# Batch 0 of a scan-then-FFN kernel taken as two tokens per partition and left unsorted, with prologue and block 0 reordered

## The chip, the cores and the metric

The kernel runs on one core of a Trainium2 chip. The metric is the device time of one execution in microseconds (us). A time is 1.7 to 2.3 us longer than the span of the same execution in the profile, because the span runs from the first to the last recorded instruction. "Fast" runs are those that are not in a slower state of the chip; all comparisons here use fast runs.

## The reference, cut to what matters

Two stages follow each other: a chunked state-space scan (batch 4, 8 heads, 768 tokens, head width 32, state width 16), and a gated feed-forward network (FFN) on its result (3072 tokens of width 256, inner width 1536).

```python
for c in range(nc):                                  # chunks in order
    cum = np.cumsum(log_a_chunk);  L = np.exp(cum_i - cum_j) * causal
    y_intra = ((C_chunk @ B_chunk.T) * L) @ x_chunk
    y_inter = (C_chunk @ state) * np.exp(cum)
    state   = np.exp(sum(log_a_chunk)) * state + (B_chunk * decay).T @ x_chunk
...
out = (np.maximum(y @ w_gate, 0) * (y @ w_val)) @ w_out
```

The kernels use chunks of 128 tokens, which gives the same result.

## The kernel before

The 3072 tokens are 12 pairs of chunks (256 tokens each, three pairs per batch) and 6 FFN blocks of 512 tokens. While block b goes through the FFN, the attention of pairs 2b+2 and 2b+3 is prepared between its matmuls. The FFN takes 12 columns f of 128: two gate and two value matmuls, a ReLU on ACT, a product h on DVE; then four output groups `fout` of 12 matmuls. A half step `gvh` takes one column for 256 tokens, a whole step `gv` for 512.

Every engine runs strictly in the order of the program text: a last pass chains each instruction to the one before it on its engine. So an instruction that waits holds up all that stands behind it on that engine. The eight PSUM banks are `y`, `Aps` (the state), `tp` (transposes) and five shared ones.

Pairs 0 to 3 are loaded "wide", with two neighbouring tokens in each partition, so that B and C come in packets of 128 bytes. Permutation matmuls then sort them back to one token per partition. The other pairs are loaded "narrow".

```python
    def sort_wide(p, engs=None, own=False):          # 8 matmuls and 2 copies for a wide pair
        ...
            for r in range(2):
                nc.tensor.matmul(out=o[:, 0:128], lhsT=order[:, i, r], rhs=s["tin"][0][r], ...)
                nc.tensor.matmul(out=o[:, 128:384]..., lhsT=order[:, i, r], rhs=s["xw"][:, r], ...)

    def tevac(p, beng, ceng):                        # B and C, transposed, leave the bank tp
        tp = s.pop("tp")
        ...
        (beng.copy if beng is nc.scalar else beng.tensor_copy)(rows(BT), tokens(0))   # first: B on ACT
        ...
        nc.vector.tensor_tensor(out=out_, in0=src.to_broadcast(shape),                # then: C on DVE
                                in1=mk.to_broadcast(shape), op=ALU.mult)
...
    # prologue: the 64x384 scan for all decays, then pair 0, then pair 1's transposes
    turn(0, True); tevac(0, nc.scalar, nc.vector); sort_wide(0, ...); G(0); gevac(0, half=False); state(0, 0)
    weights(4, 8); load(2, ...); load(3, ...); scale_bc(1, nc.vector); cast_x(1, nc.scalar); keep_warm(7)
    Dm(0); inter(0, 1); astep(0, 1); yevac(0, nc.scalar)
    turn(1, True); tevac(1, nc.scalar, nc.vector); sort_wide(1); sevac(0, 1)

    for b in range(NBLK):
        P, Q, W = 2 * b + 2, 2 * b + 3, 2 * b + 1
        ...
        for f in range(4):
            gvh(b, f, 0)
            if b == 0 and f == 0:
                G(1); gevac(1); state(1, 0); weights(8, NF); wait_for(2, 1); weights_out(0, NF)
            if f == (3 if b == 0 else 1):
                ... inter(W, 0); inter(W, 1); Dm(W); ... yevac(W, nc.scalar)
        for f in range(4):
            gvh(b, f, 1)
        for f in range(4, NF):
            gv(b, f)
            if at("scale P", 4, 4, 4): scale(P, nc.gpsimd, nc.gpsimd)     # columns for blocks 0, 1, 2 and later
            if at("turn P", 7, 6, 5):  turn(P); tevac(P, nc.scalar, nc.vector)
            if at("state P0", 9, 8, 7): state(P, 0)
            if at("turn Q", 99, 9, 8): turn(Q); tevac(Q, nc.scalar, nc.scalar)
            ...
        # output groups fout(b, 0..3), with G, gevac, Dm, yevac of P and G, gevac of Q between them
```

Of the kernel before, what the change touches and what calls it, by code (L numbers as in the profile page):

```python
# [29 lines left out]
def kernel(  # L30
# [13 lines left out]
    nc = tc.nc  # L44
# [27 lines left out]
    NWIDE = 4  # L72
    st = {}

    def wide_bc(p, qb, qc):
        b, c0 = p // PPB, 2 * (p % PPB)
        sl = slice(c0 * 128, (c0 + 2) * 128)
        bcr = raw.tile([128, NH, 2, 2, N], FP32, tag="bcr", name="bcr")
        for src, j, q in ((C, 1, qc), (B, 0, qb)):
            if (p, j) in ((0, 0), (2, 1)):  # L80
                nc.vector.memset(bcr[0:1, 0, 0, 0, 0:1], 0.0)  # L81
            q.dma_start(
                out=bcr[:, :, j].rearrange("p h r n -> p h (r n)"),
                in_=src[b, :, sl, :].rearrange("h (p r) n -> p h (r n)", r=2))
        st.setdefault(p, {})["bcr"] = bcr

    def wide_x(p, *qs):

        b, c0 = p // PPB, 2 * (p % PPB)
        sl = slice(c0 * 128, (c0 + 2) * 128)  # L90
        xr = raw.tile([128, NH, 2, D], FP32, tag="xr", name="xr")
        n = NH // len(qs)
        for k, q in enumerate(qs):
            hs = slice(k * n, (k + 1) * n)
            q.dma_start(out=xr[:, hs].rearrange("p h r d -> p h (r d)"),
                        in_=x[b, hs, sl, :].rearrange("h (p r) d -> p h (r d)", r=2))
        st.setdefault(p, {})["xr"] = xr

    def load(p, qx, qb, qc):
        b, c0 = p // PPB, 2 * (p % PPB)  # L100
        if p < NWIDE:
            wide_bc(p, qb, qc)
            wide_x(p, qx)
        else:
            xr = raw.tile([128, 2, NH, D], FP32, tag="xr", name="xr")
            bcr = raw.tile([128, 2, 2, NH, N], FP32, tag="bcr", name="bcr")
            for i in range(2):
                sl = slice((c0 + i) * 128, (c0 + i + 1) * 128)
                qx.dma_start(out=xr[:, i], in_=x[b, :, sl, :].rearrange("h s d -> s h d"))
                for src, j, q in ((B, 0, qb), (C, 1, qc)):  # L110
                    q.dma_start(out=bcr[:, i, j],
                                in_=src[b, :, sl, :].rearrange("h s n -> s h n"))
            st[p] = {"xr": xr, "bcr": bcr}

    H = S // 2
    HC = NC // 2
    a_sb = glob.tile([2 * BH, H], FP32)
    nc.sync.dma_start(out=a_sb, in_=a.rearrange("b h (w s) -> (b h w) s", w=2))
    first = const.tile([1, 2], FP32)
    nc.vector.memset(first, 0.0)  # L120
    nc.scalar.activation(first[:, 1:2], first[:, 0:1], AF.Relu)


    warm = const.tile([128, 512], BF16)
    nc.vector.memset(warm, 0.0)
    wide_bc(0, nc.scalar, nc.sync)
    wide_x(0, nc.sync, nc.scalar)
    wide_bc(1, nc.scalar, nc.sync)
    wide_x(1, nc.sync)
# [3 lines left out]
    make_identity(nc, ident)  # L133
    maskUT = const.tile([128, 1, 128], BF16)
    make_upper_triangular(nc, maskUT[:, 0], 1.0, diag=True)
# [4 lines left out]
    bd = const.tile([128, 128], BF16)  # L140
    nc.vector.memset(bd, 0.0)
    smask = const.tile([128, 2, 128], BF16)
    for k in range(4):
        nc.vector.memset(bd[32 * k:32 * k + 32, 32 * k:32 * k + 32], 1.0)
        nc.vector.memset(tmask[32 * k:32 * k + N, 0:1], 1.0)
    nc.vector.tensor_scalar(out=tmask[:, 1:2], in0=tmask[:, 0:1], scalar1=-1.0,
                            scalar2=1.0, op0=ALU.mult, op1=ALU.add)
    for t in range(2):
        nc.vector.tensor_scalar_mul(smask[:, t], bd, tmask[:, t:t + 1])
    pick = const.tile([2 * BH, 2, BH], FP32)  # L150
    pairs = identf.rearrange("p (h w) -> p w h", w=2)
    nc.vector.tensor_copy(pick[:, 1], pairs[:, 1])
    order = const.tile([128, 2, 2, 128], BF16)
    nc.gpsimd.memset(order, 0.0)
    for r in range(2):
        nc.gpsimd.tensor_copy(
            order[:, :, r].rearrange("p c (m r) -> p c m r", r=2)[:, :, :, r],
            ident.rearrange("p (c m) -> p c m", c=2))

    def keep_warm(n):  # L160
        w = bank("w")
        for _ in range(n):
            nc.tensor.matmul(out=w, lhsT=warm[:, 0:128], rhs=warm, start=True, stop=True)  # L163

    keep_warm(8)


# [15 lines left out]
    gate = const.tile([1, 4], FP32)  # L183

    def wait_for(p, j):

        nc.gpsimd.tensor_copy(gate[:, 2 * j:2 * j + 1], st[p]["bcr"][0:1, 0, j, 0, 0:1])

    wait_for(0, 1)
    weights(0, 4)  # L190


    cp = glob.tile([2 * BH, H], FP32)
    nc.vector.tensor_tensor_scan(
        out=cp, data0=a_sb, data1=zero1.to_broadcast([2 * BH, H]), initial=1.0,
        op0=ALU.mult, op1=ALU.add)
    rmid = const.tile([2 * BH, 1], FP32)
    nc.vector.reciprocal(rmid, cp[:, H - 1:H])
    nc.vector.tensor_scalar_mul(pick[:, 0], pairs[:, 0], rmid)

    def wide_decay(ps):

        d = bank("wdec", (128, len(ps), 2, 8))
        first = True
        for k, p in enumerate(ps):
            b, c0 = p // PPB, 2 * (p % PPB)
            for i in range(2):
                w, o = (c0 + i) // HC, ((c0 + i) % HC) * 128
                for r in range(2):
                    nc.tensor.matmul(  # L210
                        out=d[64 * i:64 * i + 64, k, r],
                        lhsT=cp[:, o + r:o + 128:2], rhs=pick[:, w, 8 * b:8 * b + 8],
                        start=first or (k == 0 and r == 0), stop=True,
                        tile_position=(0, 64 * i), skip_group_check=True)
                first = False
        return d

    def wide_factors(ps, d):
        f = const.tile([128, len(ps), 2, 2, 8], FP32, name="wf%d" % ps[0])
        nc.vector.reciprocal(f[:, :, 0], d)  # L220
        nc.vector.tensor_copy(f[:, :, 1], d)
        for k, p in enumerate(ps):
            st[p]["f"] = f[:, k].rearrange("p j r h -> p (j r) h")
# [22 lines left out]
    A_ps = mm.tile([128, 2, 128], FP32, tag="Aps", name="A_ps")  # L246

# [4 lines left out]

    def scale_bc(p, eng):
# [3 lines left out]
        if p < NWIDE:  # L257
            src = s["bcr"].rearrange("s (t q) j r n -> s (j r) t q n", t=2)
            f = s["f"]
        else:  # L260
            src = s["bcr"].rearrange("s i j (t q) n -> s (i j) t q n", t=2)
            f = scaleBC[:, b, c0:c0 + 2].rearrange("s c j h -> s (c j) h")
# [6 lines left out]
        if p < NWIDE:  # L269
            s["tin"] = [[bs[:, 2 * j + r] for r in range(2)] for j in range(2)]  # L270
        else:
            s["tin"] = [[bs[:, 2 * i + j] for i in range(2)] for j in range(2)]
            s["B"] = s["tin"][0]

    def cast_x(p, ceng):
# [3 lines left out]
        if p < NWIDE:  # L279
            cast(xb, s["xr"].rearrange("s h r d -> s (h r d)"))  # L280
            s["xw"] = xb.rearrange("s (h r d) -> s r h d", h=NH, r=2)
        else:
            cast(xb, s["xr"].rearrange("s i h d -> s (i h d)"))
            s["x"] = [xb[:, i * NH * D:(i + 1) * NH * D] for i in range(2)]

    def sort_wide(p, engs=None, own=False):

        s = st[p]
        bx = att.tile([128, 2, 384], BF16, tag="bx", name="bx")
        for i in range(2):  # L290
            if own and i == 0:
                o = mm.tile([128, 384], FP32, tag="y", name="bxp")
            else:
                o = bank("bxp", (128, 384))
            for r in range(2):
                nc.tensor.matmul(out=o[:, 0:128], lhsT=order[:, i, r], rhs=s["tin"][0][r],
                                 start=(r == 0), stop=(r == 1), skip_group_check=True)
                nc.tensor.matmul(
                    out=o[:, 128:384].rearrange("s (h d) -> s h d", h=NH),
                    lhsT=order[:, i, r], rhs=s["xw"][:, r],  # L300
                    start=False, stop=(r == 1), skip_group_check=True)
            eng = engs[i] if engs else nc.scalar
            (eng.copy if eng is nc.scalar else eng.tensor_copy)(out=bx[:, i], in_=o)
        s["B"] = [bx[:, i, 0:128] for i in range(2)]
        s["x"] = [bx[:, i, 128:384] for i in range(2)]
# [14 lines left out]
    def tevac(p, beng, ceng):  # L320
# [7 lines left out]
        def tokens(k, lead=""):  # L328
            src = tp[k]
            if wide:  # L330
                return src.rearrange("s r m -> s m r")
            return src.rearrange("s i m -> s (i m)")

        def rows(dst):
            dst = dst.rearrange("s i m -> s (i m)")
# [57 lines left out]
    def astep(p, i):  # L393

        c = 2 * (p % PPB) + i
        if c == NC - 1:
            return
# [260 lines left out]
```

## Time and profile before

| | before |
|---|---|
| time, two runs | 133.66 us (133.47 and 133.84) |
| span of the profiled run | 132.1 us |
| start to the first gate matmul | 13.56 us |
| from there to block 0's first output matmul | 16.88 us |
| from there to block 1's first output matmul | 19.40 us |
| from there to the end | 82.26 us |

The page's row of busy times (share of the span, instructions):

```profile
PE 125.6 (95%) x1150; PEld 83.3 (63%) x1157; DVE 90.1 (68%) x196; ACT 81.7 (62%) x177; POOL 37.6 (29%) x76
```

The page's chain that ended last, as shares of the span:

```profile
PE 58%; DVE 1%; issue 0%; DVEq 0%
```

Hardly any other engine is in the chain. The view follows it back only as far as 50.63 us (59% of the span), so for what lies before that the windows have to be read. That PE bounds the kernel there too is seen from how little it idles. The windows view, cut at the four moments of the table (stretch, its length, then busy time and instructions of each engine, granted clock, DMA share, rate):

```profile
core 0: us, PE busy (x) PEld busy (x) DVE busy (x) ACT busy (x) POOL busy (x), PEclk, DMA share, GB/s
0.00:13.56 13.56, 12.13 (x86) 6.15 (x88) 8.48 (x36) 5.40 (x11) 6.88 (x20) 1.00 0.97 140
13.56:30.44 16.88, 15.62 (x135) 9.31 (x133) 12.93 (x28) 11.03 (x27) 7.05 (x12) 1.00 1.23 178
30.44:49.84 19.40, 19.35 (x193) 13.51 (x192) 13.69 (x28) 13.89 (x32) 5.43 (x10) 1.00 0.83 115
49.84:132.10 82.26, 78.51 (x746) 54.31 (x747) 55.04 (x107) 51.42 (x111) 18.29 (x34) 1.00 0.34 60
```

Length less PE's busy time is what PE idled: 1.43, 1.26, 0.05 and 3.75 us. In the third stretch, from block 0's output to block 1's, it idles practically never. PE's longest waits besides the start are accordingly short (waits view: engine, line, what released it: us in total, times, longest):

```profile
PE gv L478 <- ACT yT L448: 0.5, 1, 0.5
PE y L424 <- DVE Sm L406: 0.3, 1, 0.3
```

What a wide pair costs on PE, from the timeline (start, us, engine, line, operation, out<-in, shapes, count). A group's end overlaps the next group's start, so the distance from one start to the next is its cost:

```profile
33.72 0.22 PE L296 MATMUL bxp<-bs,order 128*128 128x128 bf16 x1
...
34.38 1.47 PE L490 MATMUL o<-wo,h 128*128 128x256 bf16 x12
35.78 0.41 PE L435 MATMUL y<-gs,bx 128*32 128x128 bf16 x16
36.12 0.40 PE L361 MATMUL g<-CT,BT 32*128 32x256 bf16 x8
```

The sort costs 34.38 − 33.72 = 0.66 us, the 16 diagonal matmuls 0.34, and the 8 score matmuls 0.33 (the next matmul starts at 36.45).

```profile
45.05 0.37 ACT L338 COPY BT<-tp 128x256 bf16<-128x256 bf16 x1
...
45.63 0.68 DVE L352 TENSOR_TENSOR CT<-tp,tmask 128x512 bf16<-128x512 bf16 x1
```

### The profile page before, as it was taken

What the parts mean: (1) busy time and instruction counts of PE and PEld (TensorE: products, weight loads), DVE (VectorE), ACT (ScalarE), POOL (GpSimd) and SP (SyncE); (2) the same over time, 40 slices, a digit from 0 to 9 for tenths busy, and PEclk for the clock granted to TensorE, in tenths of its full rate; (3) what the DMA queues carried; (4) which work ended last, traced back from release to release, by engine and by line L of the source; (5) the groups of instructions that cost most, each with busy time, mean ns of one, the idle gap of its engine ahead of it and who ended that gap; (6) DMA issues with size and microseconds to landing.
All of it is one profiled execution on the core that took longest, in us unless ns stands there. A gap on an engine that the chain in (4) does not pass through costs nothing.

```text
span 132.1 us, 3133 instructions
## 1 busy us (share of the span) xinstructions
PE 125.6 (95%) x1150; PEld 83.3 (63%) x1157; DVE 90.1 (68%) x196; ACT 81.7 (62%) x177; POOL 37.6 (29%) x76
## 2 busy tenths in 40 slices
PE   6999979999999999999999999999999999999990
PEld 2455655547887457786557785467875577854770
DVE  5648867786478877569977568755879775687511
ACT  4046855393579784488774588744896935876410
POOL 7327374310266000293003390003750022100000
PEclk9999999999999999999999999999999999999999
DMA  3997999996877894239970279761110002200022
GB/s 73 189 183 111 181 210 194 183 144 83 108 136 141 95 118 47 87 86 122 106 83 5 79 137 116 90 64 58 52 57 0 0 0 84 79 0 0 5 88 71
DMA packets 68995, 12.10 MB, mean 92 GB/s; under 512 B 62772, under 2 KB 68980, under 8 KB 68980
## 3 DMA queue, kind: packets, MB, share of 16 engines
q1 hardware_dynamic: 62896, 8.88, 43.7%
q0 software_dynamic: 3184, 2.36, 11.9%
q10 hardware_dynamic: 2896, 0.66, 2.7%
q8 instruction: 9, 0.15, 0.5%
q14 instruction: 10, 0.05, 0.1%
HBM read 11.11 MB, written 3.15 MB: 108 GB/s over the span
## 4 chain that ended last, share of the span: by engine, by line
PE 58%; DVE 1%; issue 0%; DVEq 0%
PE o L490 20%; PE val L463 11%; PE gv L478 11%; PE gate L460 10%; PE y L435 2%; PE g L361 2%; PE A_ps L398 1%; PE tp L318 1%; PE y L424 1%; DVE h L467 0%; DVE ob L503 0%; DVEq L503 0%
## 5 line engine op out<-in xcount | busy, mean ns | idle before, releaser
L467 DVE TENSOR_TENSOR h<-r,val 128x512 bf16<-128x512 bf16 x48 | 32.6, 686 | 9.7 <-ACT r L466 8.8
L490 PE MATMUL o<-wo,h 128*128 128x256 bf16 x288 | 35.0, 273 | 0.1
L466 ACT ACTIVATE r<-gate 128x512 bf16<-128x512 f32 x48 | 28.3, 601 | 8.5 <-PE gate L460 6.2
L369 POOL TENSOR_SCALAR_AFFINE_SELECT gs<-gs 128x512 bf16<-128x512 bf16 (+1 forms) x24 | 12.2, 530 | 65.9 <-ACT gs L380 65.9
L490 PEld LDWEIGHTS <-h 128*128 128x128 bf16 x288 | 27.4, 98 | 5.1 <-issue 1.3
L463 PE MATMUL val<-yT,wv 128*128 128x512 bf16 x96 | 28.6, 379 | 0.3
L460 PE MATMUL gate<-yT,wg 128*128 128x512 bf16 x90 | 27.3, 379 | 0.3 <-ACT r L466 0.3
L482 DVE TENSOR_TENSOR h<-r,gv 128x256 bf16<-128x256 bf16 x48 | 19.9, 421 | 7.3 <-ACT r L481 6.9
L386 DVE TENSOR_TENSOR gs<-g,maskUT 128x512 bf16<-128x512 f32 x24 | 15.5, 686 | 13.0 <-issue 11.8
L481 ACT ACTIVATE r<-gv 128x256 bf16<-128x256 f32 x48 | 18.5, 385 | 2.5 <-PE gv L478 0.9
L478 PE MATMUL gv<-yT,wg 128*128 128x256 bf16 x96 | 18.4, 273 | 0.6 <-ACT yT L448 0.5
L478 PE MATMUL gv<-yT,wv 128*128 128x256 bf16 x96 | 18.3, 273 | 0.0
L463 PEld LDWEIGHTS <-wv 128*128 128x128 bf16 x96 | 9.4, 98 | 11.3
L460 PEld LDWEIGHTS <-wg 128*128 128x128 bf16 x96 | 8.8, 98 | 7.1 <-issue 0.5
L380 ACT CAST gs<-g 128x512 bf16<-128x512 f32 x12 | 7.1, 588 | 9.7 <-PE g L361 9.6
L448 ACT CAST yT<-y 128x512 bf16<-128x512 f32 x12 | 7.0, 586 | 8.2 <-PE y L435 7.1
L478 PEld LDWEIGHTS <-wg 128*128 128x128 bf16 x96 | 9.0, 98 | 2.4 <-issue 1.0
L478 PEld LDWEIGHTS <-wv 128*128 128x128 bf16 x96 | 9.4, 98 | 1.1
L264 POOL TENSOR_TENSOR bs<-bcr,scaleBC 128x256 bf16<-128x256 f32 x16 | 9.6, 623 | 0.0
L506 ACT COPY ob<-o 128x512 f32<-128x512 f32 x10 | 5.9, 586 | 4.7 <-PE o L490 4.7
L163 PE MATMUL w<-warm 128*128 128x512 bf16 x18 | 7.3, 556 | 1.3 <-DVE bcr L81 1.3
L406 DVE TENSOR_TENSOR Sm<-A_ps,smask 128x256 bf16<-128x256 f32 x20 | 8.3, 417 | 0.0
(75 smaller groups left out, 113.1 us busy)
## 6 DMA issues: line engine op xcount, KB each, us to landing
out_dram<-ob SPq DMA_DIRECT2D x10, 256.0 KB, 2.2
xr<-in_x_dram SPq DMA_DIRECT2D x17, 128.0 KB, 3.7
bcr<-in_B_dram SPq DMA_DIRECT2D x16, 64.0 KB, 3.6
bcr<-in_C_dram SPq DMA_DIRECT2D x16, 64.0 KB, 3.3
xr<-in_x_dram SPq DMA_DIRECT2D x3, 256.0 KB, 6.4
wg<-in_moe_w_gate_dram POOLq DMA_DIRECT2D x3, 256.0 KB, 5.0
wv<-in_moe_w_val_dram POOLq DMA_DIRECT2D x3, 256.0 KB, 6.2
wo<-in_moe_w_out_dram POOLq DMA_DIRECT2D x1, 768.0 KB, 11.3
```

Source lines behind the costliest of these rows:

```text
L264: eng.tensor_tensor(out=bs.rearrange("s k (q t n) -> s k t q n", q=4, t=2)[:, :, t], in0=src[:, :, t], in1=f[:, :, 4 * t:4 * t + 4].to_bro ...
L369: nc.gpsimd.affine_select(out=dst, in_=dst, pattern=[[0, n], [1, 128]], compare_op=ALU.is_ge, fill=0.0, base=0, channel_multiplier=-1)
L386: nc.vector.tensor_tensor(out=d[:, q], in0=g[q], in1=m, op=ALU.mult)
L406: nc.vector.tensor_tensor(out=n, in0=A_ps, in1=smask, op=ALU.mult)
L460: nc.tensor.matmul(out=g, lhsT=wg[:, k, fs], rhs=yT[:, k, tk], start=(k == 0), stop=(k == 1))
L463: nc.tensor.matmul(out=v, lhsT=wv[:, k, fs], rhs=yT[:, k, tk], start=(k == 0), stop=(k == 1))
L466: nc.scalar.activation(r, g, AF.Relu)
L467: nc.vector.tensor_tensor(out=fst[b][:, f], in0=r, in1=v, op=ALU.mult)
L478: nc.tensor.matmul(out=gv_[:, j], lhsT=w[:, k, fs], rhs=yT[:, k, tk], start=(k == 0), stop=(k == 1), skip_group_check=True)
L481: nc.scalar.activation(r, gv_[:, 0], AF.Relu)
L482: nc.vector.tensor_tensor(out=fst[b][:, f, u * 256:(u + 1) * 256], in0=r, in1=gv_[:, 1], op=ALU.mult)
L490: nc.tensor.matmul(out=o[:, ts % 2], lhsT=fst[b][:, f, ts * 128:(ts + 1) * 128], rhs=wo[:, f], start=(f == 0), stop=(f == NF - 1), skip_gr ...
```

## The change

The intent is to shorten the chain to the first FFN matmul. Only batch 0 (pairs 0 to 2) is loaded wide, and it is never sorted: scores, state and diagonal part are computed on the two-token layout in tiles with 64 rows, and the state is carried from chunk to chunk with one decay per chunk. A scan of 48x128 serves batch 0, so the scan of 64x384 for all batches can move into block 0. Pairs 3 and later are narrow. All loads of pairs 0 to 3 are asked for at the start. Blocks 0 and 1 take more half steps, pairs 2 and 3 are prepared later, and dummy matmuls on zeros fill places where PE would wait.

```diff
-    NWIDE = 4
+    NWIDE = PPB                                   # 3 pairs: batch 0
 ...
+    a0 = glob.tile([R, 128], FP32)
+    nc.sync.dma_start(out=a0, in_=a[0].rearrange("h (w s) -> (h w) s", s=128))
 ...
+    load(1)
     a_sb = glob.tile([2 * BH, H], FP32)
     nc.sync.dma_start(out=a_sb, in_=a.rearrange("b h (w s) -> (b h w) s", w=2))
 ...
+    load(2)
+    load(3)
 ...
-    def sort_wide(p, engs=None, own=False):
 ...
     def tevac(p, beng, ceng):
 ...
-        (beng.copy if beng is nc.scalar else beng.tensor_copy)(rows(BT), tokens(0))
         if ceng is nc.scalar:
             for t in range(2):
-                nc.scalar.mul(rows(CT[:, t]), tokens(1), tmask[:, t:t + 1])
+                nc.scalar.mul(out_[:, t], tok, tmask[:, t:t + 1])
 ...
+            nc.vector.tensor_tensor(
+                out=out_, in0=tok.unsqueeze(1).to_broadcast(shape),
+                in1=tmask.unsqueeze(2).unsqueeze(3).to_broadcast(shape), op=ALU.mult)
+        (beng.copy if beng is nc.scalar else beng.tensor_copy)(BT, tp[0])
+
+    def G_wide(p):                                 # scores: 16 matmuls
 ...
+                        lhsT=s["BT"][rows, r, 64 * i:64 * i + 64], rhs=s["CT"][rows, :, i],
+                        start=(r == 0), stop=True, tile_position=(32 * q, 64 * i),
 ...
+    def adds(p):                                   # a chunk's addition to the state: 8 matmuls
+    def carry(p, i):                               # T = T * dec + addition
+    def spread(p, i, eng):                         # T to 128 columns, masked and decayed
+    def inter_wide(p):
+    def D_wide(p):                                 # diagonal part: 32 matmuls into y and Aps
 ...
+                            lhsT=s["xb"][half, 4 * t + q, r], rhs=s["gw"][half, q, r, t],
+                            tile_position=(64 * i, 32 * q), skip_group_check=True)
 ...
+    keep_warm(16); weights(0, 4); d = factors(); keep_warm(6)          # (joined lines)
+    ... scale_wide(0, ...), transp, keep_warm(6), tevac(0, A_, V), decays(), keep_warm(8)
+    G_wide(0); adds(0); keep_warm(26)
+    gcopy(0, 0); gmask(0, 2, V, True); gcopy(0, 1); gmask(0, 0, P_)
+    spread(0, 0, V); gmask(0, 3, V, True); gmask(0, 1, V); carry(0, 0)
+    inter_wide(0); D_wide(0); yevac_wide(0, A_, V)
+    nc.vector.reciprocal(wfac[:, 0, :, :, 1:3], d[:, :, :, 1:3])
+    carry(0, 1); keep_warm(8, "tp")
+    nc.gpsimd.tensor_copy(gate[:, 0:1], wfac[0:1, 0, 0, 0, 1:2])       # POOL waits for the reciprocal
     weights(4, 8)
+    weights(8, NF); weights_out(0, NF); spread(0, 1, P_)
+    ... maskUT, bd, smask set up on POOL
+    halves(0, 0, 0, 1, 2, 3)
+    scale_wide(1, 1, V); scale_wide(1, 0, V); cast_x(1, A_); keep_warm(12)
+    turn(1, True); tevac(1, A_, V); keep_warm(12)
+    G_wide(1); adds(1); ... masks, carry(1, 0), spread(1, 0, V), carry(1, 1); keep_warm(16)
+    halves(0, 0, 4, 5); inter_wide(1); D_wide(1); yevac_wide(1, A_, V); spread(1, 1, P_)
+    scan()
+    halves(0, 0, 6, 7); halves(0, 1, 0, 1, 2, 3, 4, 5, 6, 7); gv(0, 8); decay(); gv(0, 9); gv(0, 10); gv(0, 11)
+    ... pair 2: scaled, turned after fout(0, 0), scored after fout(0, 1), applied after fout(0, 2)
+    ... pair 3: turned after fout(0, 3), scored after halves(1, 0, 0..3), applied after halves(1, 0, 4..7)
 ...
+        if b == 1:
+            halves(b, 1, 0, 1, 2, 3, 4, 5, 6, 7)
 ...
-            if at("scale P", 4, 4, 4):
+            if at("scale P", 8, 8, 4):
-            if at("turn P", 7, 6, 5):
+            if at("turn P", 9, 9, 5):
-            if at("state P0", 9, 8, 7):
+            if at("state P0", 10, 10, 7):
-            if at("state P1", 10, 10, 9):
+            if at("state P1", 11, 11, 9):
-            if at("turn Q", 99, 9, 8):
+            if at("turn Q", 99, 11, 8):
```

## The prediction

> **What bounds it now.** The engine table gives PE 95% of the span, DVE 68%, ACT 62%. The chain that ended last is almost wholly PE. From the first output projection of block 1 (49.84 us in the timeline) to that of block 5 (123.41) the blocks repeat every 17.6 to 18.8 us, of which I sum 18.5 us as PE work from start-to-start times (gate/value 10.4, output 5.25, attention 2.9). The change leaves that part and the tail alone: about 82.3 us from 49.84 to the end. So the question is whether block 1's output starts before or after 49.84. Until then: first gate matmul at 13.56, block 0's output at 30.44, and in 13.5 to 30.4 about 3 us of PE gaps. Weights ("wo" lands at about 29 us) and inputs keep the DMA engines nearly full to 30 us (windows view, 190 GB/s).
>
> **Removed.** Sorting of four pairs: 8 matmuls, about 0.65 us of warm PE each (one cold, 1.0 us, on the first chain), and evacuations of 0.5 us each on ACT and DVE. The 64x384 scan (0.95) and two small DVE steps leave the first chain; a 48x128 scan (estimate 0.4) replaces them.
>
> **Added.** For pairs 0 to 2, scores in 16 matmuls instead of 8 (estimate 0.66 us against 0.33), state adds in 16 small ones (0.35 against 0.22), 32 instead of 16 for the diagonal part (0.7 against 0.34); carries and spreads, and a DVE mask on copied scores (0.4 each). In block 0, 40 dummy matmuls at 0.056 = 2.2 us of PE. More half-width gate/value steps.
>
> **Moved.** The long scan and its followers (1.6 us of DVE) go into block 0. Pair 2 is turned, scored and applied inside block 0's output, pair 3 inside block 1's first halves; earlier they were mostly hidden in gaps before 30 us.
>
> **Estimate.** Pair 0: a smaller first load and no sort: scaled C at about 5.0 us (before 6.7), diagonal matmuls about 11 (11.99), first gate about 12.3: gain 1.2 us. Block 0: pair 1's scaling on DVE stands behind four h products, so it is only turned at 15.2 to 15.7, and applied at 19.6 to 20.3 (before 17.2). DVE then does the scan, ten products and the 1.37 us of reciprocals, behind which two ACT copies and three ReLUs stand in order. Block 0's first output group ends near 31.1 against 31.75. Then 1.1 us more PE work than before stands in the path, and PE stalls: about 0.5 us for pair 2's spread and masks, and 2 us around pair 3, whose four score banks take nearly all five shared banks between the halves. Block 1's output then starts at 50 to 52.4 us: later by 0 to 2.5. I lean less than fully on the stalls. Predicted 134.8 us, 80% range 132.3 to 137.0. Chances: faster by over 2% 0.06, within 2% 0.70, slower by over 2% 0.24.
>
> The Trainium skill, page "TensorE: Matmul & The Clock Gate", says the array starts at half rate and warms after about 3.4 us of sustained work. This trace agrees in kind: 512-column matmuls 0.42 us apart until 10.2, about 0.22 after. The dummies serve that.
>
> **What would show it.** First gate matmul 12 to 12.8. Block 0's output first at 29 to 30. PE waiting for DVE or ACT in block 0, before pair 2's inter matmuls, and around pair 3's scores. Blocks 2 to 5 spaced as before.
>
> **What would make it wrong.** The array warming at about 7 us, or pair 0 ready earlier than 11: then gain 1 to 2 us. Eight 64x32 tiles overlapping better than estimated. Dummies filling only time idle anyway. Weights for columns 4 to 8 landing after 18.4 us: slower still.

## The result, and the profile after

The kernel after takes 142.38 us (142.24 and 142.52), the one before 133.66. The ratio is 1.068 (95% interval 1.056 to 1.080): 6.8% slower. A ratio is the mean time of one kernel's fast runs over that of the other's of the same rounds, so it is not quite the ratio of the medians that are quoted. This matters a little here, because the kernel before falls on about 132.3 or about 133.7 us from run to run. For that reason each experiment below gives its ratio beside its time.

The row of busy times and the chain that ended last, after:

```profile
PE 127.9 (91%) x1333; PEld 90.4 (64%) x1333; DVE 93.1 (66%) x205; ACT 78.6 (56%) x179; POOL 44.1 (31%) x91
```

```profile
PE 71%; DVE 12%; POOL 6%; issue 3%; ACT 2%; DMA 2%; SPq 1%; ACTq 0%; DVEq 0%; POOLq 0%
```

The span grew by 8.3 us. PE is busy 2.3 us longer (127.9 − 125.6) and idle 6.0 us longer (12.5 instead of 6.5). Here the view follows the chain back almost to the start (97% of the span), and DVE and POOL are in it: before 50 us PE waits for them. The two rows of shares cover different stretches, so they can't be compared figure by figure. The windows after, cut at the same four events (columns as before):

```profile
0.00:13.42 13.42, 10.91 (x151) 9.09 (x152) 6.06 (x26) 3.68 (x8) 6.49 (x22) 1.00 0.95 166
13.42:32.94 19.52, 16.33 (x199) 11.77 (x199) 15.24 (x38) 10.35 (x27) 11.64 (x23) 1.00 0.95 123
32.94:57.73 24.79, 21.47 (x240) 15.23 (x238) 17.97 (x39) 13.37 (x33) 7.69 (x12) 1.00 0.78 105
57.73:140.40 82.67, 79.17 (x750) 54.28 (x747) 53.79 (x105) 51.16 (x113) 18.24 (x34) 1.00 0.32 59
```

Lengths change by −0.14, +2.64, +5.39 and +0.41 us. PE's idle time is now 2.51, 3.19, 3.32 and 3.50 us. So nothing was won before the first gate matmul, block 0 lost 2.6 us, and the stretch with block 0's output and block 1's columns lost 5.4. The 5.4 are 2.1 us more of PE's busy time (21.47 against 19.35, since work moved there) and 3.3 more of idle time. The rest is almost unchanged: from block 1's output to block 5's it is 73.40 us before (the timeline has block 5's at 123.24; the prediction's 123.41 is from the view of the chain) and 73.77 after.

PE's waits after:

```profile
PE A_ps L503 <- DVE Sm L511: 1.5, 1, 1.5
PE y L447 <- POOL gs L370: 1.1, 1, 1.1
...
PE gv L583 <- DVE h L587: 0.9, 1, 0.9
PE y L433 <- DVE T L410: 0.7, 1, 0.7
PE tp L323 <- DVE bs L279: 0.7, 1, 0.7
...
PE gv L583 <- DMA wv<-in_moe_w_val_dram: 0.3, 1, 0.3
```

All but the last are waits for an engine that was busy with, or waiting for, something ahead in its own queue. The second one comes from POOL (timeline after, POOL alone):

```profile
13.60 0.18 POOL L654 COPY gate<-wfac 1x1 f32<-1x1 f32 x1 [3.00 <-DVE wfac L651]
13.72 0.79 POOL L191 DMA_DIRECT2D wg<-in_moe_w_gate_dram  x1
...
19.75 1.48 POOL L665 TENSOR_SCALAR smask<-bd,tmask 128x128 bf16<-128x128 bf16 x2
21.20 1.14 POOL L370 TENSOR_TENSOR gs<-gs,wmask 128x512 bf16<-128x512 bf16 x1
```

POOL waits 3.00 us for a reciprocal that stands behind pair 0's evacuation on DVE. Then it asks for five weight loads (3.9 us), and sets up masks that pair 3 is the first to need. Only at 21.20 does it mask pair 1's scores, for which PE waits until about 22.4.

The other half lies at the end of block 1's columns (timeline after):

```profile
54.48 0.68 DVE L342 TENSOR_TENSOR CT<-tp,tmask 128x512 bf16<-128x512 bf16 x1
...
55.20 0.37 ACT L345 COPY BT<-tp 128x256 bf16<-128x256 bf16 x1 [1.36 <-DVE CT L342]
...
55.46 1.09 ACT L571 ACTIVATE r<-gate 128x512 bf16<-128x512 f32 x2
...
56.71 0.42 DVE L511 TENSOR_TENSOR Sm<-A_ps,smask 128x256 bf16<-128x256 f32 x1
...
57.18 0.27 PE L503 MATMUL A_ps<-xb,bs 128*128 128x256 bf16 x1 [1.48 <-DVE Sm L511]
```

ACT idles 1.36 us until DVE has copied C out of `tp`; only then can it copy B and go on to two ReLUs; DVE waits for the first of these (0.94 us), and the state copy `Sm` behind it comes late; PE waits 1.48 us. Over the whole run ACT waits so for 8.0 us (waits view, ACT):

```profile
ACT BT L345 <- DVE CT L342: 8.0, 6, 2.3
```

Before, the copy of B came first in every such pair, as the timeline in "More of the kernel before" shows for one.

What the new arithmetic costs on PE (timeline after, pair 2):

```profile
36.12 0.42 PE L357 MATMUL g<-CT,BT 32*64 32x256 bf16 x16
36.47 0.24 PE L391 MATMUL y<-xb,bs 64*32 64x64 bf16 x8
36.86 1.47 PE L595 MATMUL o<-wo,h 128*128 128x256 bf16 x12
...
39.84 0.24 PE L447 MATMUL y<-gs,xb 64*32 64x128 bf16 x4
...
40.19 1.48 PE L595 MATMUL o<-wo,h 128*128 128x256 bf16 x12
```

Sixteen score matmuls cost 0.35 us, and the 32 diagonal ones 0.35, about 11 ns each. Each group has twice the matmuls of before at nearly the same cost. Pair 2 has only eight additions, since the last chunk of a batch needs none; the next matmul starts 0.39 us after them, but they are busy for only 0.24. Pair 1's sixteen cost 0.19 (18.30 to 18.49). The sort's 0.66 us is gone. So the arithmetic of a wide pair is cheaper on PE. What is left as causes are the order of work, the dummies and the new work of the other engines; the experiments separate them.

Last, the prologue (timeline after, PE):

```profile
9.36 2.89 PE L182 MATMUL w<-warm 128*128 128x128 bf16 x26 [0.43 <-ACT gs L374]
...
12.30 0.24 PE L447 MATMUL y<-gs,xb 64*32 64x128 bf16 x4
...
13.42 0.38 PE L583 MATMUL gv<-yT,wg 128*128 128x256 bf16 x2 [0.15 <-DVE yT L457]
```

Pair 0's masks are done at 10.88 us, but PE is in its 26 dummies until 12.09: 2.73 us for 26 is 105 ns each, half rate. The diagonal matmuls start at 12.30.

### The profile page after: what moved, and what is told of

It reads as the page before. It is cut to its first block, busy times and chain, and to the rows that moved or that the text cites. A ratio compares the mean times of both kernels' runs of the same rounds, so it can differ in the third digit from the quotient of the medians.

```text
span 140.4 us, 3539 instructions
## 1 busy us (share of the span) xinstructions
PE 127.9 (91%) x1333; PEld 90.4 (64%) x1333; DVE 93.1 (66%) x205; ACT 78.6 (56%) x179; POOL 44.1 (31%) x91
## 4 chain that ended last, share of the span: by engine, by line
PE 71%; DVE 12%; POOL 6%; issue 3%; ACT 2%; DMA 2%; SPq 1%; ACTq 0%; DVEq 0%; POOLq 0%
PE o L595 21%; PE gv L583 13%; PE gate L565 11%; PE val L568 11%; DVE h L587 3%; PE w L182 3%; DMA xr<-in_x_dram 2%; PE g L466 2%; PE y L540 2%; PE tp L323 2%; PE A_ps L503 1%; DVE gs L370 1%; PE y L529 1%; POOL smask L665 1%; DVE h L572 1%
## 5 line engine op out<-in xcount | busy, mean ns | idle before, releaser
L572 DVE TENSOR_TENSOR h<-r,val 128x512 bf16<-128x512 bf16 x40 | 26.6, 684 | 8.9 <-ACT r L571 8.2
L587 DVE TENSOR_TENSOR h<-r,gv 128x256 bf16<-128x256 bf16 x64 | 25.7, 418 | 7.4 <-ACT r L586 6.8
L586 ACT ACTIVATE r<-gv 128x256 bf16<-128x256 f32 x64 | 24.2, 384 | 6.6 <-PE gv L583 2.8
L583 PE MATMUL gv<-yT,wg 128*128 128x256 bf16 x128 | 24.5, 273 | 1.5 <-DVE h L587 0.9
L571 ACT ACTIVATE r<-gate 128x512 bf16<-128x512 f32 x40 | 22.8, 604 | 3.8 <-PE gate L565 3.5
L583 PE MATMUL gv<-yT,wv 128*128 128x256 bf16 x128 | 24.4, 273 | 0.3 <-DMA wv<-in_moe_w_val_dram 0.3
L568 PE MATMUL val<-yT,wv 128*128 128x512 bf16 x80 | 23.8, 379 | 0.0
L491 DVE TENSOR_TENSOR gs<-g,maskUT 128x512 bf16<-128x512 f32 x18 | 11.6, 686 | 10.9 <-issue 9.1
L182 PE MATMUL w<-warm 128*128 128x128 bf16 x110 | 10.8, 271 | 1.5 <-DVE tmask L156 1.1
L182 PEld LDWEIGHTS <-warm 128*128 128x128 bf16 x110 | 9.2, 124 | 1.8 <-DVE tmask L156 1.0
```

The source lines that it names most:

```text
L182: nc.tensor.matmul(out=w, lhsT=warm, rhs=warm, start=True, stop=True)
L491: nc.vector.tensor_tensor(out=d[:, q], in0=g[q], in1=m, op=ALU.mult)
L568: nc.tensor.matmul(out=v, lhsT=wv[:, k, fs], rhs=yT[:, k, tk], start=(k == 0), stop=(k == 1))
L571: nc.scalar.activation(r, g, AF.Relu)
L572: nc.vector.tensor_tensor(out=fst[b][:, f], in0=r, in1=v, op=ALU.mult)
L583: nc.tensor.matmul(out=gv_[:, j], lhsT=w[:, k, fs], rhs=yT[:, k, tk], start=(k == 0), stop=(k == 1), skip_group_check=True)
```

## The experiments

The theory after reading the traces was: the loss is made of several waits behind in-order engines (POOL's chain, the scan, pair 1's scaling, pairs 2 and 3, block 1's preparation), and each can be taken back by moving the queued work. Rivals were: the unsorted arithmetic itself costs PE more; the dummies cost time; and, found later, the order of the two readers of `tp`. Seventeen kernels ran, all with correct results. "First out 0/1" below is the start of block 0's / block 1's first output matmul in the profiled run (after: 32.94 / 57.73). Diffs are against the kernel after unless said otherwise. Kernels of one group (e1 to e4; e5 to e7 and c1; e8, b1, c2 and c3; c4, c4v and c5; c6 and c6n) ran on one chip beside runs of the kernel before. Gains in us against the kernel after are differences of medians from different chips; the ratios are free of that, but they carry the two times of the kernel before. "A hit" means that the time fell where the expectation put it.

The prologue varies from run to run. The kernels after, e2, e5 and e6 have the same program on PE, ACT and DVE up to the first gate matmul, yet in their profiled runs it starts at 13.42, 13.76, 13.90 and 14.03 us. So a "first out" is good to about 0.6 us, and stretches that begin at the first gate matmul are the safer comparison.

**e1_no26**, the 26 dummies taken away:

```diff
-    keep_warm(26)
```

> The changed kernel without the 26 dummy matmuls ahead of pair 0's diagonal part. Theory A (order: the loss is made of waits behind work that stands too early in an engine's queue): the masks are done at 10.9 us, the dummies end at 12.1, so the diagonal matmuls start at about 11.0 instead of 12.3 and all that follows moves up: about 141.2 us, 1.2 less. Rival (the dummies are needed to warm the array): the array stays at half rate past 12 us, the first gate matmuls are 0.2 us apart instead of 0.11, and the time stays at 142 or more.

Measured: 142.44 us, ratio 1.070 (1.064 to 1.076), a miss: nothing gained. Pair 0 was indeed 1.6 us earlier (diagonal 10.67) and the first gate matmul 1.1 us earlier, but at half rate (timeline, PE):

```profile
12.34 0.64 PE L583 MATMUL gv<-yT,wg 128*128 128x256 bf16 x2
12.77 0.63 PE L583 MATMUL gv<-yT,wv 128*128 128x256 bf16 x2
...
15.27 0.38 PE L583 MATMUL gv<-yT,wv 128*128 128x256 bf16 x2
```

Two matmuls take 0.43 us (12.77 − 12.34) where the kernel after takes 0.21, until about 15.1. First out 0 was 32.94, the same. The dummies bought the clock that they cost; the rival reading was right about the time.

**e2_setup_late**, POOL's set-up of masks for pair 3 moved behind pair 1's work:

```diff
-    make_upper_triangular(nc, maskUT[:, 0], 1.0, diag=True)
-    ... bd, smask (POOL)
 ...
     spread(1, 1, P_)
+    make_upper_triangular(nc, maskUT[:, 0], 1.0, diag=True)
+    ... bd, smask (POOL)
```

> The changed kernel with the later pairs' masks built on POOL after pair 1's masking instead of before it. Theory A: POOL masks pair 1 by about 20.6 instead of 22.35, the diagonal matmuls of pair 1 start at about 21.0, no wait of 1.1 us before them, 141.1 us. Rival (the unsorted arithmetic and the dummies are simply more PE work): the wait is filled by another and the time stays within 0.3 of 142.4.

Measured: 140.94 us, ratio 1.058 (1.051 to 1.064); first out 31.64 / 56.43. PE's wait of 1.1 us for POOL is gone. From the first gate matmul to block 0's output it took 17.88 us instead of 19.52. A hit: about 1.4 us of POOL's chain were on the critical path.

**e3_scan_early**, the long scan ahead of pair 0's decays, its load ahead of pair 1's:

```diff
-    load(1)
     a_sb = ...
     nc.sync.dma_start(out=a_sb, ...)
+    load(1)
 ...
+    scan()
     decays()
 ...
-    scan()
```

> The changed kernel with the 64x384 scan and its three followers in DVE's idle time at 6 to 8.8 us (its load moved ahead of pair 1's). Theory A: the wait of 0.9 us of PE for h products at 25 us goes, and 2.3 us of DVE leave block 0: block 0's output starts 1 to 1.5 us earlier, 141.0 us. Rival (DVE throughput does not matter, PE work or DMA does): no change.

Measured: 141.94 us, ratio 1.066 (1.059 to 1.072); first out 31.82 / 56.61. The profiled run was the 1.1 us shorter that was expected, the median of four runs only 0.4, and the interval of its ratio overlaps that of the kernel after. So a gain is not resolved by the times. In the trace, PE's wait of 0.9 us for h products at 25 us is gone, as expected, and from the first gate matmul to block 0's output it took 18.46 us instead of 19.52; its wait for `wv` grew from 0.3 to 0.8. This stays half settled.

**e4_scale1_early**, pair 1's reciprocal and scaling ahead of pair 0's evacuation on DVE:

```diff
     gmask(0, 1, V)
+    nc.vector.reciprocal(wfac[:, 0, :, :, 1:3], d[:, :, :, 1:3])
+    scale_wide(1, 1, V)
+    scale_wide(1, 0, V)
     carry(0, 0)
```

(The same three lines are taken away further down.)

> The changed kernel with pair 1 scaled on DVE in its idle time at 10.9 to 12.8 us, ahead of the first h products. Theory A: pair 1 is turned about 0.9 us earlier, but POOL masks it no earlier (22.35), so the gain is taken back by the wait before its diagonal matmuls: within 0.3 of 142.4. A rival that makes DVE's late scaling of pair 1 the cause of block 0's loss expects 141.5.

Measured: 141.02 us, ratio 1.058 (1.051 to 1.065); first out 31.68 / 56.47. A miss in the good direction. I had thought of pair 1's transposes only. But the reciprocal is also what POOL waits for: its gate copy came at 11.23 instead of 13.60, so the weights, the set-up and pair 1's mask (18.70 instead of 21.20) all came about 2.4 us earlier. It is the same wait of PE that e2 removes, cut at another link.

**e5_blk1**, block 1's preparation of pairs 4 and 5 spread over its second halves, as before, not packed into the last four columns:

```diff
-            halves(b, 1, 0, 1, 2, 3, 4, 5, 6, 7)
+            scale(P, P_, P_); scale(Q, P_, P_)
+            halves(b, 1, 0, 1, 2, 3)
+            turn(P); tevac(P, A_, V)
+            halves(b, 1, 4, 5)
+            state(P, 0)
+            halves(b, 1, 6, 7)
 ...
-            if at("state P1", 11, 11, 9):
+            if at("state P1", 9, 9, 9):
-            if at("turn Q", 99, 11, 8):
+            if at("turn Q", 99, 9, 8):
```

> The changed kernel with block 1's preparation of pairs 4 and 5 spread over its second halves as before the change did, instead of packed into its last four steps. Theory A: the wait of 1.5 us of PE for a DVE state product ahead of block 1's output goes: 140.9 us, 1.5 less. Rival (later waits take the gain back, or PE work is the cause): within 0.4 of 142.4.

Measured: 141.28 us, ratio 1.059 (1.053 to 1.066). From block 0's output to block 1's it took 23.64 us instead of 24.79. A hit in kind, 1.1 us where 1.5 was expected.

**e6_pairs23**, pair 2 turned after column 9 of block 0 and scored after the first output group; pair 3 turned after pair 2's masks and scored before the last output group (the calls moved, none changed):

```diff
+    gv(0, 9)
+    turn(2); tevac(2, A_, V)
+    gv(0, 10); gv(0, 11); fout(0, 0); foevac(0, 0)
+    G_wide(2); adds(2); ... masks
+    turn(3); tevac(3, A_, V)
+    fout(0, 1) ... fout(0, 2); inter_wide(2); D_wide(2); yevac_wide(2, A_, V)
+    G(3); gevac(3); state(3, 0)
+    fout(0, 3); halves(1, 0, 0, 1); astep(3, 1); inter(3, 1); Dm(3)
```

> The changed kernel with pair 2 turned during the last gate/value steps of block 0 and scored after the first output group, two output groups ahead of its diagonal part, and pair 3 turned and scored inside block 0's output: the places they had before the change. The unsorted arithmetic stays. Theory A: the waits of 1.0 us before pair 2's state and diagonal matmuls, of 1.0 around pair 3's scores and of 0.5 for its yT go: 139.9 us, 2.5 less. Rival (the unsorted arithmetic is the cost): within 0.5 of 142.4.

Measured: 141.09 us, ratio 1.059 (1.052 to 1.065). It gained 1.3 us, well short. Its trace shows why: the copy of pair 2's C now stood on DVE ahead of block 0's last products, and that of B behind it on ACT, so the first output group, from 33.79 on, itself stalled twice for h products, 0.98 and 0.31 us. This was the first hint of the order in `tevac`.

**e7_nodummy**, block 0's 48 dummies taken away:

```diff
-    keep_warm(8, "tp")
-    keep_warm(12)
-    keep_warm(12)
-    keep_warm(16)
```

> The changed kernel without the 48 dummy matmuls after pair 0's diagonal part (2.6 us of PE at full clock). Theory A: they fill time in which PE would wait for DVE or POOL, so without them it is 142.4 less at most 0.5. Rival (dummies are work on the critical path): 140 to 141. If the array cools down for want of them, gate matmuls 0.2 us apart show it and the time is over 142.4.

Measured: 142.17 us, ratio 1.067 (1.059 to 1.074); first out 32.95 / 57.75. As expected in time: the dummies cost nothing net. Yet they are not idle filling only. Without them the granted clock fell (windows of e7; the last three numbers are clock, DMA share, rate):

```profile
20.00:22.00 2.00, 1.29 (x7) 0.92 (x8) 1.63 (x6) 0.39 (x1) 1.86 (x5) 0.66 1.45 206
22.00:24.00 2.00, 1.71 (x40) 1.22 (x39) 1.01 (x4) 0.76 (x2) 2.00 (x4) 0.50 1.65 204
```

**c1_order** is e2 to e6 together.

> The late masks, the early scan, the early scaling of pair 1, pairs 2 and 3 and block 1 as in the separate runs, all at once; arithmetic, loads and dummies as in the changed kernel. Theory A: the gains add, save that the first and third both act on POOL ahead of pair 1's mask: 1.4 + 1.1 + 0.7 + 2.5 + 1.5 = 7.2, so 135 to 136.5. Rival (PE work of the unsorted arithmetic): no lower than 139.

Measured: 137.15 us, ratio 1.030 (1.022 to 1.038); first out 29.93 / 52.28. The five alone gained 1.44 + 0.44 + 1.36 + 1.10 + 1.29 = 5.6 us, together 5.2. That is above the 135 to 136.5 expected and well below the rival's 139. Order explains over half of the loss, but 4 us were still missing.

**e8_evac**, the copy of B ahead of that of C again, as in the kernel before:

```diff
+        (beng.copy if beng is nc.scalar else beng.tensor_copy)(BT, tp[0])
         tok, out_ = tp[1], CT
 ...
-        (beng.copy if beng is nc.scalar else beng.tensor_copy)(BT, tp[0])
```

> The changed kernel with BT copied out of the shared bank before CT again, as before the change; nothing else. Theory B (found in the trace after: the two copies read one bank and are kept apart, so with CT first ACT stands still for DVE, 8.0 us in all, and the ReLUs stand behind it): the wait of 1.5 us ahead of block 1's output goes and blocks 2 to 5 lose their 0.1 us each: 140.6 us, 1.8 less. Rival (idle ACT costs nothing here): within 0.4 of 142.4.

Measured: 140.30 us, ratio 1.060 (1.058 to 1.062). ACT's wait for C is gone from its list, and PE's wait of 1.5 us before block 1's state is 0.4. A hit: one line, 2.1 us by the medians. The ratio falls less, by 0.8% or about 1.1 us, from 1.068 to 1.060; on that chip the kernel before was mostly at its lower time (median 132.39). A third way, from the first gate matmul to the end of the two profiled runs, gives 126.98 and 125.15 us, 1.8 less.

**b1_swap** is the test from the other side: the kernel before, with only that copy moved down (also in the branch, cut here, in which ACT copies both, as in the kernel after).

```diff
-        (beng.copy if beng is nc.scalar else beng.tensor_copy)(rows(BT), tokens(0))
 ...
         nc.vector.tensor_tensor(out=out_, in0=src.to_broadcast(shape),
                                 in1=mk.to_broadcast(shape), op=ALU.mult)
+        (beng.copy if beng is nc.scalar else beng.tensor_copy)(rows(BT), tokens(0))
```

> The kernel before with this one part of the change: CT copied out ahead of BT. Theory B: ACT stands still for DVE as in the changed kernel, 0.5 to 1.5 us slower than before, 134 to 135. Rival: no difference, 133.4.

Measured: 135.27 us, ratio 1.020 (1.014 to 1.026; whether over or under 2% is unclear, that it is slower is not). By the medians it is 2.9 us over the kernel before on the same chip (132.39), more than expected. The prologue is not the reason: from the first gate matmul to the end the profiled runs take 118.54 us before and 120.91 here, 2.4 more. The wait of the kernel after appears in it (waits view, ACT):

```profile
ACT BT L354 <- DVE CT L352: 8.2, 6, 1.5
```

**c2_order_evac** is c1 and e8 together.

> c1_order with BT first. Theory B: of the waits left in c1_order, 1.3 us in the first output group and 0.5 before pair 3's scores come from ACT standing behind DVE's CT: 135.3 us, 1.8 less than c1_order. Rival: 137.1 as c1_order.

Measured: 135.00 us, ratio 1.018 (1.013 to 1.023), a hit; first out 29.74 / 49.84. Block 1's output starts at 49.84, as in the kernel before, and PE has no wait over 0.5 us left after 10 us. (The profiled run, 133.84 us, was its fastest, and its first gate matmul was early, at 12.85; the others took 134.7 to 135.4.) So six moves of queued work took back 7.4 of 8.7 us by the medians, 5.0 of 6.8% by the ratios, with all of the new arithmetic still in place.

The remaining kernels look for a version that beats both.

**c3_shape** is c2 with block 0 in the order of the kernel before (pair 1 turned straight after pair 0, applied after four halves) and without block 0's dummies:

```diff
-    keep_warm(8, "tp")
+    cast_x(1, A_); turn(1, True); tevac(1, A_, V)
 ...
-    halves(0, 0, 0, 1, 2, 3)
-    ... keep_warm(12) twice
+    halves(0, 0, 0, 1)
+    G_wide(1); adds(1); ... mask on POOL, carry(1, 0), spread(1, 0, V), masks, carry(1, 1)
+    halves(0, 0, 2, 3); inter_wide(1); D_wide(1)
+    halves(0, 1, 0, 1, 2, 3); gv(0, 4) ... gv(0, 8)
```

(Pair 1's spread thereby moves ahead of two of its masks, and the load of `wo` behind POOL's mask.)

> c2_order_evac with block 0 in the order of the kernel before: pair 1 turned right after pair 0's diagonal part, two half steps before its scores, full-width steps from the fifth on, no dummies after pair 0. The unsorted arithmetic stays. Theory A: block 0's output at about 28.5 us, block 1's at 48, 130.5 to 132 us, faster than before. Rival (the unsorted arithmetic costs at least what sorting did): 133.5 or more.

Measured: 136.08 us, ratio 1.029 (1.025 to 1.033), a miss; the time is one that the rival allowed, so it took c4 to tell them apart. DVE's spread of pair 1 met POOL's mask (timeline of c3):

```profile
16.84 1.15 POOL L370 TENSOR_TENSOR gs<-gs,wmask 128x512 bf16<-128x512 bf16 x1 [1.02 <-ACT gs L374]
...
17.16 1.11 DVE L420 TENSOR_TENSOR Sm<-T,decm 128x256 bf16<-128x256 f32 x1
```

The spread takes 0.4 to 0.5 us where no POOL mask runs for most of it (0.42 in the kernel after); here 1.11, ending 0.28 us after POOL's mask (18.27 and 17.99). Two masks and a carry stand behind it, and PE waited 1.93 us until 19.45. Then the granted clock fell to 0.50 from about 20 to 23.3 us, and 256-column matmuls went at half rate. The Trainium skill, page "SBUF — State Buffer", section "Who interferes with whom", says that a DVE instruction with two inputs in SBUF contends with a POOL instruction that reads SBUF, and that the ports which the two share are an exclusive lock. The traces agree: DVE ends 0.28 us after POOL here, equally in the kernel after (38.53 and 38.81, for a DVE mask that took 0.88 instead of 0.41), and in e6 (39.17 and 39.45, for a spread of 1.10). DVE masks with one input in PSUM kept their 0.69 us beside POOL's mask (after, 36.73 to 38.02).

**c4_block0** is c3 with the work placed around that: masks that read PSUM first on DVE, the spread behind them; two more half steps and ten dummies ahead of pair 1's application; weights 4 to 8 asked for right after pair 0's decays (6.4 us was expected; in the trace POOL came to it at 8.10):

```diff
     decays()
+    weights(4, 8)
 ...
     gmask(1, 0, P_)
+    gmask(1, 3, V, True)
     carry(1, 0)
     spread(1, 0, V)
-    gmask(1, 3, V, True)
 ...
-    halves(0, 0, 2, 3)
+    halves(0, 0, 2, 3, 4, 5)
+    keep_warm(10)
```

(Likewise for pair 2's masks.)

> c3_shape with pair 1's PSUM masks first on DVE while POOL works on its own mask, four half steps and 10 dummies (not two half steps) between its scores and its diagonal part, and weights 4 to 8 asked for at 6.4 us. Theory C (c3_shape lost in block 0 because PE stood 1.9 us behind DVE operands that POOL's mask slows from 0.41 to 1.1 us, and the array then cooled down): no matmul at half rate after 15 us, block 0's output at 28.5 to 29.5 us, 132 to 133.5. Rival (unsorted arithmetic): 135 to 136 as c3_shape.

Measured: 132.96 us, ratio 0.998 (0.991 to 1.006), a hit; first out 29.31 / 48.98. The spread takes 0.52 us again, and the clock stays up. That the unsorted arithmetic is the cost is thereby refuted, since all of it is still there. The four changes of c4 came together, so what each is worth is not shown.

**c4v_dve** is c4 with pair 1's POOL mask on DVE instead:

```diff
-    gmask(1, 0, P_)
+    gmask(1, 0, V)                                # behind gmask(1, 3, V, True)
```

> c4_block0 with pair 1's first mask on DVE instead of POOL. Theory C: DVE's spread of pair 1 takes 0.42 us and its SBUF masks 0.41 each, so nothing is lost by taking the work from POOL: within 0.4 of c4_block0. Rival (DVE's slow operands have another cause than POOL's mask): the spread still takes about 1.1 us and the time is 0.5 or more over c4_block0.

Measured: 133.29 us, ratio 0.999 (0.993 to 1.005), as expected: the spread takes 0.43 us. Once the order is right, it is the same who masks.

**c5_prologue** is c4 with a shorter first chain:

```diff
-        nc.gpsimd.tensor_scalar_mul(ends, onew, cp0[:, 127:128])
+        nc.vector.tensor_scalar_mul(ends, onew, cp0[:, 127:128])
 ...
-    scan()
     decays()
     weights(4, 8)
-    keep_warm(8)
     G_wide(0)
     adds(0)
-    keep_warm(26)
+    keep_warm(16)
 ...
     yevac_wide(1, A_, V)
+    scan()
```

(Two small steps behind the scan also move from DVE to POOL.)

> c4_block0 with pair 0's chain freed: the chunk ends on DVE instead of behind POOL's cast, no 8 dummies ahead of the scores, 16 instead of 26 behind them, the scan behind pair 1's evacuation. If waits ahead of pair 0's scores cost what they show (1.6 us), the first gate matmul is at 11 to 11.6 us and the time 1 us under c4_block0; if the array is then cold, the gain is half of that or none.

Measured: 131.85 us, ratio 0.989 (0.983 to 0.995); first gate matmul at 11.90, first out 28.25 / 47.93. A hit in time, 1.1 us under c4 on the same chip; the first gate matmul came later than the 11 to 11.6 expected, and the gate matmuls ran at half rate until about 13.6.

**c6_fill** is c5 with two half steps moved into the gap after pair 1's diagonal part:

```diff
     yevac_wide(1, A_, V)
+    halves(0, 0, 6, 7)
     scan()
```

(Further down, columns 6 and 7 of the second half become half steps too.)

> c5_prologue with two more half steps (columns 6 and 7, first half) behind pair 1's diagonal matmuls, which need only pair 0. They fill the 1.0 us in which PE waits for pair 1's evacuation by DVE: that wait goes, 131.0 us, 0.9 less, about 2% faster than before. Rival (DVE, which then has more half products to make, gives it back later): 131.6 or more.

Measured: 131.00 us, the median of five fast runs (130.87 to 132.30; a sixth, of 134.82, was slow and is left out), ratio 0.987 (0.981 to 0.992). That is the time expected. It is the best version, 1.35% under the kernel before. The interval excludes no change, but the gain is under the 2% that count as a difference here. The gain over c5, which ran on another chip, is 0.85 us by the medians and 0.2% by the ratios, so it is not resolved by these runs. The wait of 1.0 us is gone from PE's list. Its windows (profiled run, 131.99 us), to be held against those of before and after:

```profile
0.00:12.18 12.18, 9.57 (x128) 7.23 (x129) 7.89 (x33) 3.70 (x9) 9.03 (x26) 1.00 0.98 164
12.18:28.09 15.91, 15.17 (x168) 10.09 (x169) 13.71 (x33) 10.71 (x28) 8.53 (x21) 1.00 1.18 165
28.09:47.63 19.54, 19.26 (x236) 14.98 (x235) 15.70 (x36) 13.92 (x34) 7.38 (x12) 1.00 0.90 115
```

PE idles 0.74 and 0.28 us in the second and third stretch, where the kernel after idled 3.19 and 3.32. Its 129.7 us span holds 122.6 us of PE work, 3.0 less than before.

**c6n_nodummy** is c6 without its 16 and 10 dummies.

```diff
-    keep_warm(16)
-    keep_warm(10)
```

> c6_fill without the 26 dummies behind pair 0's scores. From e1: the array then warms later, the first gate matmuls are 0.2 us apart for longer, and what is gained ahead of them is lost: 131 to 132, no faster than c6_fill. If the dummies are only ballast: 0.5 less than c6_fill.

Measured: 131.91 us, ratio 0.990 (0.985 to 0.995), as expected. Its gate matmuls ran at half rate until about 15.9 us. Against c6, on the same chip, it is 0.9 us slower by the medians, but the runs overlap and the difference is within the intervals.

## Why the prediction was right or wrong

The direction was the likelier of the two changes that it named (24% slower against 6% faster), but it put 70% on "within 2%", and 142.38 us lies far above its range of 132.3 to 137.0.

**Right.** PE bounds the kernel, and the part from block 1's output on hardly changed: 73.40 and 73.77 us from block 1's output to block 5's. PE waits in block 0, before pair 2's inter matmuls (0.7 us) and around pair 3 were named beforehand, and the trace has them. The late weights for columns 4 to 8, named as a danger, are there too: PE waits 0.3 us for `wv` in the kernel after and 1.35 us, until 20.71, in e7.

**Wrong: the added arithmetic.** It said scores 0.66 us, state 0.35 and diagonal 0.7 us per pair. Scores and diagonal cost 0.35 us each, pair 1's sixteen state additions 0.19. Tiles that use different parts of the array overlap far better than I had estimated: 0.35 us for the 32 diagonal matmuls, not 0.7. The Trainium skill, page "TensorE: Matmul & The Clock Gate", section "Measured speedup vs the span model", gives the span of a pack of tiles as one matmul's time and about 4 ns for each further tile. An estimate from it and from the 54 ns that half of a warm 256-column matmul takes in this trace (109 ns from start to start) is 54 + 7 × 4 = 82 ns for eight tiles, 0.33 us for the 32 diagonal matmuls; the trace has 0.35, so it agrees. I had not used it. This error was on the safe side, so it makes the other errors larger.

**Wrong: the prologue's gain of 1.2 us.** Pair 0 was nearly as early as predicted: its masks were done at 10.88, against diagonal matmuls "about 11". The first gate matmul came at 13.42 instead of 12.3 because I had not costed the 26 dummies at half rate: 2.73 us, ending 1.2 us after the masks. But e1 shows that they are no plain loss: without them the first gate matmul starts at 12.34 and nothing is gained, because the array is then at half rate until 15.1. The Trainium skill, page "TensorE: Matmul & The Clock Gate", section "What's actually happening", says that the array runs at 1.2 GHz until about 3.4 us of sustained work and at 2.4 after. The traces agree in kind: dummies of 128 columns come 105 ns apart before 12.1 us, and gate matmuls of 256 columns, twice the work, 109 ns apart from 13.42 on. In e1 the earlier start was paid back whole in clock; in c5, with 16 dummies and a shorter chain, the first gate matmul came 1.8 us earlier than in c4 (11.90 against 13.73) and 1.1 us of that stayed.

**Wrong: the step "PE stalls: about 0.5 us for pair 2's spread and masks, and 2 us around pair 3", and "I lean less than fully on the stalls".** This is the term of the sum that was mis-sized, and it was missing altogether for block 0. PE's idle time grew by 6.0 us, not 2.5. Block 0's output came at 32.94, not at 29 to 30, and block 1's at 57.73, not at 50 to 52.4. The prediction let pair 1 be applied at 19.6 to 20.3; it was at 22.39, behind POOL's mask. The experiments show what the term should have held:

- POOL's chain, from a reciprocal on DVE over five weight issues and a mask set-up to pair 1's mask: 1.4 us (e2 and e4, each cutting it at one link). I had followed DVE's order in block 0, not POOL's.
- Block 1's preparation packed into its last four columns: 1.1 us (e5).
- Pairs 2 and 3 inside the output groups and first halves: 1.3 us (e6).
- The scan in block 0: 0.4 us by the medians, 1.1 us by the spans of the profiled runs, not resolved (e3).
- The order of the two copies out of `tp`: 1.1 to 2.1 us, by the way of comparing (e8), and 2.0% when put into the kernel before alone (b1_swap).

**Missed altogether: that last one.** The prediction does not mention it, though it stands in the diff. From pair 2 on both copies read one PSUM bank. The Trainium skill, page "PSUM — Partial Sum Buffer", section "PSUM bank collisions raise a hardware error", says that two engines must not be in the same bank and quadrant at once, reads included, and that the compiler's scheduler puts a dependency between them. The trace agrees as to the dependency: B waits for C for 8.0 us in six waits. With B first, DVE stands at most behind a copy of 0.37 us, and no copy of B waits for C in the kernel before. With C first, ACT stands until DVE has worked off its products, and ACT's ReLUs, which PE and DVE need, stand behind it. The work is the same in both orders; only who waits differs.

c2 undoes all five together, and keeps the new arithmetic, the dummies and, but for one small load moved forward, the load scheme: 135.00 us, 7.4 of the 8.7 us that were lost (5.0 of 6.8% by the ratios). What remained, up to the kernel before, closed with block 0's order in c4 (132.96), and the shorter prologue of c5 (131.85) and the filled gap of c6 (131.00) then went below it. So the unsorted arithmetic is not what cost 6.8%: with it, one order of work is 6.8% slower than the kernel before, and another 1.35% faster. Whether the 1.35% comes from leaving out the sort is not shown, because the sorted arithmetic was never run in c6's order and with its shortened prologue.

**Still open.** Why e3 gained 1.1 us in its profiled run and 0.4 in the median. Why the kernel before has two times, 1.4 us apart, among its fast runs. A likely cause stands in two traces whose programs are the same up to this point (first the kernel before, then b1_swap):

```profile
5.95 1.89 PE L163 MATMUL w<-warm 128*128 128x512 bf16 x4
...
5.61 1.04 PE L163 MATMUL w<-warm 128*128 128x512 bf16 x4
```

The same four dummies go at half rate in the one and at full rate in the other, and the first gate matmul starts at 13.56 and 12.19, 1.37 us apart. It is not shown, since no run of the kernel before at the lower time was profiled. And whether c6's dummies or its last two moved half steps are worth anything: the differences from c6n and c5 are inside the intervals.

## What to carry to other kernels

After a rewrite, compare the order on every engine, not only on the one that bounds: a queue behind a reciprocal, a weight issue or a set-up becomes PE's wait several steps later. Two engines that read one PSUM bank need an order, and the one with the more urgent work behind it should read first. A better idea and a worse order can come in one diff; take the order back first, then judge the idea, and give the old version the better order too.

## What the Trainium skill lacked or had wrong

- "PSUM — Partial Sum Buffer" states the bank rule, but not that the order of two readers decides which in-order engine stands, nor its price: 8.2 us of ACT's waits and 2.0% of the time in b1_swap, 1.1 to 2.1 us in e8.
- "TensorEngine Tiling (Array Packing)", section "Instruction Overhead", gives about 60 cycles of overhead per matmul, and "TensorE: Matmul & The Clock Gate", section "Wait — 56ns, not 53.3ns?", says that start-to-start is never below about 25 ns. Neither says there that this does not hold across tiles, as the second page's "Measured speedup vs the span model" implies. Here 32 matmuls dealt out over eight tiles took 0.35 us, 11 ns each.
- "TensorE: Matmul & The Clock Gate" puts the return to half rate after an idle window of about 3.4 us. In c3 the clock fell to 0.50 with no idle stretch after 16 us longer than 1.93 us and PE busy for 2.07 of the 4 us from 16 to 20 us. The page says that many short idles between groups of matmuls can make the clock swing too, but it gives no busy share below which it falls.
- "TensorE: Matmul & The Clock Gate" warns that the clock events of a trace have been unreliable, but no page says that the granted clock in the records leaves out the first warm-up: it reads 1.00 in the first window of the kernel after, in which 128-column matmuls came 105 ns apart. The later falls, in c3 and e7, are in it.
